# Weight splits of the first segments moved to ScalarE and GpSimd, and a third set of score operands, in a four-layer attention and Fourier kernel

## The chip, the core and the metric

One NeuronCore of a Trainium2 chip runs the whole program. Its engines each follow their own instruction stream and wait for each other through semaphores: TensorE (PE) multiplies matrices into PSUM, VectorE (DVE) and ScalarE (ACT) work on SBUF and PSUM, GpSimd (POOL) on SBUF only, and SyncE (SP) issues the DMAs. The metric is the device time of one execution in microseconds, the lower the better; the kernel is compared by the median of several executions.

## What is computed

`x` has 2048 rows of 512 values. Two kinds of layers alternate, twice each, and every layer adds to `x`:

```python
x = x + A(layernorm(x)); x = x + B(layernorm(x))
x = x + A(layernorm(x)); x = x + B(layernorm(x))

def A(x):            # 32 heads of width 16; the sequence in 4 segments of 512 rows
    for s in range(4):
        qs, ks, vs = the segment's q, k, v          # x @ wq, x @ wk, x @ wv
        a_dot = softmax(qs @ ks.T / 4 + causal mask) @ vs
        a_mem = (phi(qs) @ M) / (phi(qs) @ z + 1e-6)  # phi(t) = t+1 if t>0 else exp(t)
        outs.append(g * a_mem + (1 - g) * a_dot)      # g = sigmoid(beta)
        M = M + phi(ks).T @ vs;  z = z + sum(phi(ks))
    return concat(outs) @ wo

def B(x):            # Fourier mixing, real part
    a, b = x @ dft_hid_re.T, x @ dft_hid_im.T
    return dft_seq_re @ a - dft_seq_im @ b
```

## The kernel before

**Numbers.** Matrix products with float32 operands are made of float16 halves. Each weight matrix is scaled by a power of two taken from its largest magnitude and split into a high half (rounded to float16) and a low half (what the rounding lost); a product is then three matmuls, high by high, high by low and low by high (`mm3`). The scale needs a chain of its own: `absmax` reduces along the row on VectorE, `scales` transposes the result on TensorE, takes the maximum over partitions, and spreads it with a second matmul. `split` makes the halves: ScalarE writes the high one from `src` and the scale `s`, and VectorE the low one with a single scalar_tensor_tensor, (`src` × `s`) − high.

**Attention.** The 32 heads are cut into four groups of eight (`NG`), and the work is numbered by `i`, segment by segment and group by group: 4 groups × 4 segments × 2 layers = 32. For each `i`: `s_p` projects q and k with the group's weights; `t_split` makes halves of them and sends these through DRAM into the operand tiles `qst[i % NR]` and `kst[i % NR]`; `s_x` multiplies q by k for the row maxima, which VectorE takes from PSUM (`t_max`, in the profile the operation whose output is named `junk`, with `mx` behind it); a transpose of `mx` ends them, and four small DMAs put the negative maxima into `qst` as extra rows; `s_st` makes the scores, `t_sel` exponentiates them on ScalarE and masks them with an affine select on GpSimd; `s_av` multiplies them by v, from `vt[i % NR]`; `s_m` divides and merges (`t_merge`, with a round trip of denominators and reciprocals through DRAM), and `s_mem` keeps the memory. `NR` = 2, so two sets of operand tiles: `t_split` waits for the scores of group `i` − 2 before it writes the operands of group `i`, and `s_v` for that group's memory update and attention sum before it writes `vt`.

**Constant rows.** Rows 32 to 63 and 96 to 127 of `qst` and `kst` are filled once (`s_k`), `qst` with zeros by GpSimd, `kst` by VectorE: zeros, and an added column `pf` that puts 8192 in two rows of each half, which multiply the maxima's rows of `qst`. `t_split` and `s_x` overwrite the other rows of these blocks.

**Weights at the start.** `y` is the tile in which the Fourier layers sum their result; before that its pieces serve as staging room for the weights. The DMAs of the query and key weights of group 0 follow those of the first four tiles of `x`. `s_w` then goes through the groups: reductions and scales of query and key, the factors `f_q`, `f_k`, `f_k2` and `f_s`, the split of the query and the key weights, and a store of each to DRAM (`wqkv`), from which later segments load them. In group 0 it then waits for the layer norm of the first four tiles (`L`), issues all other weight loads and takes the scale of the value weights (`WL`); the value weights come last in each group. `s_wo` loads the output weights after `WL`, and the Fourier hidden weights (`wd`) after group 3's query and key (`W`); it makes the scales and 4 + 8 splits, after which `WO` lets the output projection (`s_o`), the hidden transform (`s_ab`) and the loads of the sequence matrices (`s_r`) begin.

**The order.** All of these are Python generators that yield what they need next: an engine, tiles, and slots from a shared pool of 2 KB per partition (`NW` = 50 slots, named `w` in the profile; PSUM banks are `b`; `g` holds the normalised, transposed rows). A planner (`Plan`) keeps an estimate of every engine's and tile's time with written-down costs, and always takes the step that can start first, with fixed priority among equals: so the instruction order of every engine is settled when the program is built, and any change of a cost, a slot count or a wait can change the order of everything behind it. `tt` chooses between VectorE and GpSimd for a tensor_tensor: it adds 8 ns per element to VectorE's planned free time and 2 to GpSimd's, and takes the smaller. Slots have limits per kind; at most three query or key weight tiles (`wt`) and two value tiles (`wv`) are held at once.

Every engine call passes through one helper, so nearly all instructions in the profile stand under line 247; they are told apart by tile names.

Of the kernel before, what the change touches and what calls it, by code (L numbers as in the profile page):

```python
# [1 line left out]

# [19 lines left out]
HG = H // NG  # L22
NP = HG // 2
LAYERS = 2
NW, NB = 50, 2
PAIRS = NT // 2
CHUNKS = [2] * 8
LATE = [(5, 0, 8), (6, 0, 4), (7, 0, 4), (5, 8, 12), (6, 4, 8), (7, 4, 8), (5, 12, 16), (6, 8, 12), (7, 8, 12),
# [8 lines left out]
RESERVE = dict(G=500.0, Y=1000.0, V=0.0, A=0.0)  # L37
BATCH = 4
FIRST = "cc", "craw"
NR = 2  # L40


class Plan:
# [99 lines left out]
    def op(self, eng, name, args, kw):  # L143
# [7 lines left out]
        if eng == "T":  # L151
            n, w = out[0].free_size(), aps[1]
            slow = 4 if w.dtype == F32 else 1
            c = n / 2.4 * slow + (18 if w.dtype == F32R else 3)
            cols = n * slow * w.partition_size() / 128
            mode, unit = "m", 0
            if name == "matmul" and out[0].partition_size() == 32:
                mode, unit = "v", out[0].start_partition() // 32
            elif w.partition_size() <= 64:
                mode, unit = "h", w.start_partition() // 64  # L160
        elif eng == "A":
            c = n / 1.2 + (52 if src else 93) + (93 if any(a.free_size() == 1 for a in ins) else 0)
        elif eng == "V":
            c = 68 + n / 0.96
            if name == "reciprocal":
                c = 68 + n * 6.25
            elif name == "scalar_tensor_tensor" and out[0].dtype == F32:
                c += 60
            elif name == "tensor_copy" and out[0].dtype == F16:
                c = 68 + n / 1.92  # L170
            elif name == "tensor_scalar" and out[0].dtype == F32:
                c = 68 + n / (0.87 if src else 1.32)
        elif eng == "G":
            c = 127 + n * 0.915 if name == "affine_select" else 96 + n * 2.2
# [79 lines left out]
def body(ctx: ExitStack, tc: tile.TileContext, x, wq, wk, wv, wo, beta, wd, cs, out):  # L254
# [38 lines left out]

    load(0, 0)
    load(0, 1)
    macc = const.tile([128, NG, 2, 4, 32], F32, name="macc")
    pl.fine[macc.tensor.name] = 256
    jp = macc[:, 0, 0].rearrange("p j d -> p (j d)")
# [86 lines left out]
    def flat(t):  # L385
        return t.rearrange("p a b -> p (a b)")

    def s_w():
        def part(n, g):
            i = 2 * g + n if n < 2 else 8  # L390
            yield need("A", tag="wv" if n == 2 else "wt")
            w = sb("wv" if n == 2 else "wt", F16, (128, 2, KT, 128))
            yield from split(w, stage[g][n], scl[:, i:i + 1])
            yield need("Y", w)
            Y.dma_start(wqkv[g][n], w)
            wnow[n, g] = w
            done.add(("W", n, g))

        for g in range(NG):
            for n in range(2):  # L400
                yield need("V", stage[g][n])
                absmax(2 * g + n, flat(stage[g][n]))
            yield from scales(2 * g, 2 * g + 2)
# [4 lines left out]
            yield from part(0, g)  # L408
            yield from part(1, g)
            if g == 0:  # L410
                yield gate(*[("L", 0, t) for t in range(TT)])
                Y.dma_start(gb[:, 0, :], beta)
                for j in range(NG):
                    load(j, 2)
                    if j:
                        load(j, 0)
                        load(j, 1)
                for j in range(NG):
                    yield need("V", stage[j][2])
                    V.tensor_reduce(vm[:, j:j + 1], flat(stage[j][2]), axis=AX.X, op=OP.max,  # L420
                                    apply_absolute_value=True)
                V.tensor_reduce(amax[:, 8:9], vm, axis=AX.X, op=OP.max)
                yield from scales(8, 9)
                done.add("WL")
            yield from part(2, g)

    def s_wo():
        wos = y[:, 12:16, :]
        yield gate("WL")
        Y.dma_start(wos, wo.rearrange("(t p) n -> p t n", p=128))  # L430
        yield gate(("W", 0, 3), ("W", 1, 3))
        wds = y[:, 0:8, :].rearrange("p (t e) n -> p t (e n)", e=2)
# [12 lines left out]
        V.tensor_scalar(f_o, inv[:, 8:9], inv[:, 9:10], 2.0 ** 9, op0=OP.mult, op1=OP.mult)  # L445
        V.tensor_scalar(f_y, inv[:, 10:11], 2.0 ** 9, None, op0=OP.mult)
        for k in range(KT):
            yield from split(w_o[:, :, k], wos[:, k], scl[:, 9:10])
        for e, s in enumerate((scl[:, 10:], sneg)):
            for k in range(KT):  # L450
                yield from split(w_d[:, :, k, 512 * e:512 * e + 512], wds[:, k, 512 * e:512 * e + 512], s)
        done.add("WO")

    def s_k():
# [3 lines left out]
            V.tensor_copy(f, t)  # L458
            V.tensor_scalar(f, f, scale, None, op0=OP.mult)

        pz = const.tile([128, 1], I32, name="pz")
        pf = const.tile([128, 1], F32, name="pf")
        yield need("V")
        V.tensor_scalar(pz, pi, 62, None, op0=OP.bitwise_and)
        V.tensor_copy(pf, pz)
        V.tensor_scalar(pf, pf, 62.0, 8192.0, op0=OP.is_equal, op1=OP.mult)
# [732 lines left out]
```

## Time and profile before

| | |
|---|---|
| runs of the kernel | 1785.94, 1790.37, 1789.98 us; median 1789.98 |
| the profiled execution | 1784.85 us |
| its span, first to last instruction | 1783.1 us |
| mean granted TensorE clock | 0.979 |
| busy: PE, DVE, ACT, POOL | 1676.0, 1111.9, 898.7, 723.1 us (94, 62, 50, 41% of the span) |
| DMA | 242.44 MB, 48.3% of 16 engines' span on SP's queue |

How to read the rows: in the summary by slices each digit is the busy share of one fortieth of the span, in tenths (for PEclk the granted clock, in tenths of full speed). In the views of single instructions the columns are start, duration (both in us), engine, line, operation, output and inputs by tile name with buffer numbers left out, shape, and count, then in brackets the idle time of the engine before it and what ended that. In the rows of groups the numbers behind the bar are busy time in us and the mean of one in ns, then the engine's idle time before these instructions. Matmul ends are modelled, and rows that stand for several instructions give the time from the first one's start to the last one's end.

### The profile page before, as it was taken

What the parts mean: (1) busy time and instruction counts of PE and PEld (TensorE: products, weight loads), DVE (VectorE), ACT (ScalarE), POOL (GpSimd) and SP (SyncE); (2) the same over time, 40 slices, a digit from 0 to 9 for tenths busy, and PEclk for the clock granted to TensorE, in tenths of its full rate; (3) what the DMA queues carried; (4) which work ended last, traced back from release to release, by engine and by line L of the source; (5) the groups of instructions that cost most, each with busy time, mean ns of one, the idle gap of its engine ahead of it and who ended that gap; (6) DMA issues with size and microseconds to landing.
All of it is one profiled execution on the core that took longest, in us unless ns stands there. A gap on an engine that the chain in (4) does not pass through costs nothing.

```text
span 1783.1 us, 32611 instructions
## 1 busy us (share of the span) xinstructions
PE 1676.0 (94%) x11029; PEld 731.7 (41%) x11029; DVE 1111.9 (62%) x3440; ACT 898.7 (50%) x1563; POOL 723.1 (41%) x1154
## 2 busy tenths in 40 slices
PE   3877899999999999999899998999999999999999
PEld 1432444443444444444444443444344434444444
DVE  7797865867596687455577757555756476533222
ACT  2547668666557667733437663565445544531000
POOL 3225455546454455543435544353624343331000
PEclk8888899999999999999999999999999999999999
DMA  7345645565465554345774772355424453227104
GB/s 195 99 124 134 176 118 140 163 176 149 124 182 150 148 129 134 106 123 165 221 222 156 199 181 73 95 139 149 122 81 119 131 133 87 83 92 230 53 0 136
DMA packets 240984, 242.44 MB, mean 136 GB/s; under 512 B 129776, under 2 KB 152304, under 8 KB 240816
## 3 DMA queue, kind: packets, MB, share of 16 engines
q1 hardware_dynamic: 240816, 240.35, 48.3%
q8 instruction: 87, 1.43, 0.3%
q14 instruction: 81, 0.66, 0.1%
HBM read 152.96 MB, written 63.70 MB: 122 GB/s over the span
## 4 chain that ended last, share of the span: by engine, by line
PE 59%; DVE 12%; DMA 12%; issue 5%; POOL 5%; ACT 4%; SPq 3%; POOLq 0%; DVEq 0%; ACTq 0%
PE b L247 59%; ACT w L247 4%; DVE junk L247 4%; POOL w L247 4%; DMA w<-w 3%; DVE w L247 3%; SPq L247 3%; DMA dc<-den 2%; DMA w<-rec 1%; DMA w<-in_cs_dram 1%; DMA den<-w 1%; DVE cam L247 1%; DMA w<-x 1%; DVE y L247 1%; DMA rec<-dc 1%
## 5 line engine op out<-in xcount | busy, mean ns | idle before, releaser
L247 PEld LDWEIGHTS <-w 128*128 128x128 f16 x4992 | 464.9, 98 | 624.6 <-issue 118.4
L247 PE MATMUL b<-w,w 128*128 128x512 f16 x3072 | 707.9, 380 | 5.8 <-POOL w L247 3.7
L247 POOL TENSOR_TENSOR w<-w,w 128x512 f16<-128x512 f32 (+1 forms) x317 | 381.2, 1208 | 372.9 <-ACT w L247 236.0
L247 ACT ACTIVATE w<-b,fac 128x512 f32<-128x512 f32 (+1 forms) x728 | 420.9, 657 | 207.8 <-PE b L247 193.1
L247 DVE CUSTOM_DVE_ANT_0 junk<-b,cmask 128x128 bf16<-128x128 f32 (+3 forms) x1024 | 438.4, 484 | 50.4 <-PE b L247 49.7
L247 POOL TENSOR_SCALAR_AFFINE_SELECT w<-w 128x128 f32<-128x128 f32 (+2 forms) x704 | 244.1, 359 | 364.4 <-ACT w L247 358.7
L247 DVE SCALAR_TENSOR_TENSOR y<-b,fyu,y 128x512 f32<-128x512 f32 x232 | 173.3, 747 | 215.9 <-PE b L247 214.5
L247 ACT ACTIVATE w<-b 128x512 f32<-128x512 f32 (+1 forms) x240 | 137.5, 599 | 176.1 <-PE b L247 171.1
L247 ACT ACTIVATE w<-w,csc 128x512 f16<-128x512 f32 (+1 forms) x256 | 181.7, 721 | 56.5 <-DVE csc L247 42.6
L247 PE MATMUL b<-g,w 128*128 128x512 f16 x768 | 186.7, 386 | 8.8 <-issue 5.3
L247 PE MATMUL b<-w,vt 128*32 128x512 f32 (+3 forms) x2048 | 176.7, 446 | 3.8 <-POOL w L247 2.8
L247 PE MATMUL b<-wd,w 128*128 128x512 f16 x768 | 179.9, 380 | 0.0
L247 DVE SCALAR_TENSOR_TENSOR w<-b,w 128x512 f16<-128x512 f32 x128 | 87.9, 687 | 131.5 <-ACT w L247 128.0
L247 ACT ACTIVATE w<-w 128x512 f16<-128x512 f32 (+1 forms) x144 | 90.1, 631 | 157.0 <-DVE w L247 116.1
L247 PE MATMUL b<-kst,qst 62*128 62x128 f16 (+3 forms) x1024 | 128.9, 307 | 15.3 <-DVE mx L247 7.1
L247 PE MATMUL b<-qst,kst 64*128 64x512 f16 (+3 forms) x1024 | 117.5, 305 | 8.6 <-ACT w L247 4.0
L247 PE MATMUL b<-w,g 128*128 128x128 f16 x1536 | 98.0, 221 | 9.6 <-DMA w<-w 4.4
L247 PEld LDWEIGHTS <-g 128*128 128x128 f16 x1536 | 88.8, 99 | 25.9 <-issue 16.0
L247 PEld LDWEIGHTS b<-w,vt 128*32 128x32 f32 x2048 | 53.9, 109 | 94.9 <-issue 53.2
L247 PE MATMUL b<-wo,w 128*128 128x512 f16 x384 | 89.8, 390 | 1.1 <-ACT w L247 0.9
L247 DVE TENSOR_REDUCE cam<-w 128x1 f32<-128x512 f32 x128 | 81.4, 675 | 11.2 <-DMA w<-in_cs_dram 11.0
L247 DVE DVE_READ_ACCUMULATOR2_ANT mx<- 128x1 f32 x1024 | 84.0, 82 | 0.0
(103 smaller groups left out, 841.0 us busy)
## 6 DMA issues: line engine op xcount, KB each, us to landing
w<-in_cs_dram SPq DMA_DIRECT2D x128, 256.0 KB
cc<-w SPq DMA_DIRECT2D x128, 256.0 KB
w<-cc SPq DMA_DIRECT2D x128, 256.0 KB
w<-w SPq DMA_DIRECT2D x96, 256.0 KB
d<-w SPq DMA_DIRECT2D x128, 128.0 KB
w<-rec SPq DMA_DIRECT2D x56, 256.0 KB
w<-in_x_dram SPq DMA_DIRECT2D x32, 256.0 KB
qst<-d SPq DMA_DIRECT2D x64, 128.0 KB
```

The source lines that it names most:

```text
L247: r = f(*args, **kw)
```

## The change

Five parts go together.

1. `split2` is new. ScalarE writes the high half, then scales `src` in place; the low half is a plain subtraction, handed to VectorE or GpSimd by `tt`. It takes the place of `split` everywhere but for group 0's query and key weights: 10 splits of query, key and value weights, 4 of the output weights and 8 of the Fourier weights.
2. The order of `s_w`: group 1's query and key weights are loaded beside group 0's, before the layer norm's transposes are issued; one chain of `scales` serves both groups; the four splits of groups 0 and 1 come first. All value weights and the query and key weights of groups 2 and 3 are loaded after the layer norm; their eight reductions come together, with one chain of `scales` for them and the value weights, and then eight splits in a fixed order.
3. `s_wo` waits for group 1's maxima (`("X", 1)`) as well before it loads the output weights.
4. `NR` goes from 2 to 3: a third `qst`, `kst` and `vt`. The room comes from the DMA scratch of the program, set to 1024; `NW` goes from 50 to 52.
5. The constant rows of `kst` are a memset on GpSimd with a float32 that holds two float16 8192; the column `pf` and VectorE's work for it go. Rows of these blocks that used to be zero now hold 8192. The planner's cost of a GpSimd memset or iota is written down as 80 + 0.9 per element.

```diff
-NW, NB = 50, 2
+NW, NB = 52, 2
...
-NR = 2
+NR = 3
+K8192 = struct.unpack("<f", b"\x00\x70" * 2)[0]
...
-            c = 127 + n * 0.915 if name == "affine_select" else 96 + n * 2.2
+            c = 127 + n * 0.915 if name == "affine_select" else 80 + n * 0.9 if name in ("memset", "iota") else 96 + n * 2.2
...
     load(0, 0)
     load(0, 1)
+    for n in range(2):
+        load(1, n)
...
-        dg = rg("dg", 3, F32, (128, 4))
+        dg = rg("dg", 3, F32, (128, 8))
...
+    def split2(o, src, s):
+        yield need("A", src, s)
+        A.activation(o[:, 0], src, AF.Copy, scale=s)
+        A.activation(src, src, AF.Copy, scale=s)
+        yield need("VG", o, src)
+        tt(o[:, 1], src, o[:, 0], OP.subtract)
+
     def s_w():
-        def part(n, g):
+        def part(n, g, how):
...
-            yield from split(w, stage[g][n], scl[:, i:i + 1])
+            yield from how(w, stage[g][n], scl[:, i:i + 1])
...
+        for g in range(2):
+            for n in range(2):
+                yield need("V", stage[g][n])
+                absmax(2 * g + n, flat(stage[g][n]))
+        yield from scales(0, 4)
+        for n in range(2):
+            yield from part(n, 0, split)
+        factors(0)
+        factors(1)
+        for n in range(2):
+            yield from part(n, 1, split2)
+        yield gate(*[("L", 0, t) for t in range(TT)])
+        for g in range(NG):
+            load(g, 2)
+        for g in range(2, NG):
+            for n in range(2):
+                load(g, n)
+        Y.dma_start(gb[:, 0, :], beta)
+        for g in range(NG):
+            yield need("V", stage[g][2])
+            V.tensor_reduce(vm[:, g:g + 1], flat(stage[g][2]), axis=AX.X, op=OP.max, apply_absolute_value=True)
+        V.tensor_reduce(amax[:, 8:9], vm, axis=AX.X, op=OP.max)
+        for g in range(2, NG):
+            for n in range(2):
+                yield need("V", stage[g][n])
+                absmax(2 * g + n, flat(stage[g][n]))
+        yield from scales(4, 9)
+        done.add("WL")
+        factors(2)
+        factors(3)
+        for x in ((2, 0), (0, 2), (1, 2), (2, 1), (2, 2), (0, 3), (1, 3), (2, 3)):
+            yield from part(*x, split2)
...
     def s_wo():
-        yield gate("WL")
+        yield gate("WL", ("X", 1))
...
-            yield from split(w_o[:, :, k], wos[:, k], scl[:, 9:10])
+            yield from split2(w_o[:, :, k], wos[:, k], scl[:, 9:10])
...
-                yield from split(w_d[:, :, k, 512 * e:512 * e + 512], wds[:, k, 512 * e:512 * e + 512], s)
+                yield from split2(w_d[:, :, k, 512 * e:512 * e + 512], wds[:, k, 512 * e:512 * e + 512], s)
...
         for i in range(NR):
-            for t, e in ((qst[i], G), (kst[i], V)):
+            for t, c in ((qst[i], 0.0), (kst[i], K8192)):
                 for a in range(2):
                     r = slice(64 * a + 32, 64 * a + 64)
-                    yield need(e.key)
-                    e.memset(t[r].rearrange("r p n -> r (p n)").bitcast(F32), 0.0)
-                    if e is V:
-                        yield need("V", pf)
-                        V.tensor_scalar(t[r], t[r], pf[r], None, op0=OP.add)
+                    yield need("G")
+                    G.memset(t[r].rearrange("r p n -> r (p n)").bitcast(F32), c)
...
-    nc = _bacc.Bacc("TRN2", target_bir_lowering=False, num_devices=1)
+    nc = _bacc.Bacc("TRN2", target_bir_lowering=False, num_devices=1, dynamic_dma_scratch_size=1024)
```

More of the change, by code (lines that the diff above doesn't have):

```diff
@@ L1 @@
+import struct
 from contextlib import ExitStack
@@ L397, in part, with factors @@
             done.add(("W", n, g))
[L399 to L403, printed above, removed]
+        def factors(g):
             for f, n, e in ((f_q, 0, -10), (f_k, 1, -10), (f_k2, 1, 12)):
@@ L407, in s_w @@
                             op0=OP.mult, op1=OP.mult)
[L408 to L425, printed above, removed]
+        for g in range(2):
[30 more added lines that the diff above has]
+            yield from part(*x, split2)
     def s_wo():
         wos = y[:, 12:16, :]
-        yield gate("WL")
+        yield gate("WL", ("X", 1))
         Y.dma_start(wos, wo.rearrange("(t p) n -> p t n", p=128))
@@ L459, in bits @@
             V.tensor_scalar(f, f, scale, None, op0=OP.mult)
[L461 to L466, printed above, removed]
         for i in range(NR):
-            for t, e in ((qst[i], G), (kst[i], V)):
+            for t, c in ((qst[i], 0.0), (kst[i], K8192)):
                 for a in range(2):
                     r = slice(64 * a + 32, 64 * a + 64)
-                    yield need(e.key)
-                    e.memset(t[r].rearrange("r p n -> r (p n)").bitcast(F32), 0.0)
-                    if e is V:
-                        yield need("V", pf)
-                        V.tensor_scalar(t[r], t[r], pf[r], None, op0=OP.add)
+                    yield need("G")
+                    G.memset(t[r].rearrange("r p n -> r (p n)").bitcast(F32), c)
             done.add(("QI", i))
```

## The prediction

> **What bounds the kernel now.** I read the page's summary by slices first, then the busy time by stage, then the first 230 us instruction by instruction.
>
> ```profile
> PE   3877899999999999999899998999999999999999
> DVE  7797865867596687455577757555756476533222
> PEclk8888899999999999999999999999999999999999
> ```
>
> Each digit is a 44.6 us slice. TensorE is below nine tenths, and its granted clock below full, in the first five slices; from then on it is the bound nearly everywhere. The next view puts numbers to it: the columns are the stretch, its length, then the busy time of PE, weight loads, DVE, ACT and POOL, the granted clock and the DMA share.
>
> ```profile
> 0.00:20.00 20.00, 1.21 (x4) 0.72 (x5) 17.40 (x47) 5.13 (x7) 12.93 (x20) 1.00 0.59 145
> 20.00:45.00 25.00, 13.79 (x92) 8.31 (x92) 16.31 (x66) 4.18 (x8) 2.46 (x2) 0.73 0.85 231
> 45.00:90.00 45.00, 40.17 (x320) 18.85 (x321) 32.97 (x130) 24.66 (x45) 10.71 (x24) 0.89 0.39 105
> 90.00:135.00 45.00, 34.67 (x241) 15.28 (x241) 41.45 (x164) 20.28 (x39) 12.13 (x26) 0.85 0.39 116
> 135.00:180.00 45.00, 33.10 (x224) 11.40 (x224) 30.76 (x75) 33.50 (x61) 23.91 (x44) 0.85 0.52 137
> 180.00:225.00 45.00, 37.90 (x265) 18.50 (x265) 37.60 (x145) 27.69 (x49) 21.16 (x31) 0.85 0.63 178
> 225.00:1740.00 1515.00, 1475.76 (x9708) 640.99 (x9705) 923.40 (x2803) 783.22 (x1360) 639.80 (x1008) 1.00 0.48 134
> 1740.00:1784.00 44.00, 39.41 (x183) 17.68 (x181) 12.01 (x16) 0.00 (x0) 0.00 (x0) 1.00 0.41 138
> ```
>
> Length less PE's busy time is PE's idle time: 18.8, 11.2, 4.8, 10.3, 11.9 and 7.1 us, together 64.1 us before 225 us, against 39.2 us in the 1515 us after it and 4.6 at the end. Busy time times (1 − clock) bounds what the lower clock cost in the five stretches from 20 us: 3.7, 4.4, 5.2, 5.0 and 5.7, together 24 us. So about 88 us are lost in the first eighth of the span, and that is where this change works. What is late there is told by the transposes that end each group's maxima (one per group of eight heads) and by group 1's weights.
>
> ```profile
> 56.55 0.40 PE L247 MATMUL b<-identf,mx 128*32 128x128 f32 x1 [3.70 <-DVE mx L247]
> 98.22 0.39 PE L247 MATMUL b<-identf,mx 128*32 128x128 f32 x1 [3.91 <-DVE mx L247]
> 129.14 0.28 PE L247 MATMUL b<-identf,mx 128*32 128x128 f32 x1 [0.39 <-DVE mx L247]
> 157.14 0.28 PE L247 MATMUL b<-identf,mx 128*32 128x128 f32 x1 [1.52 <-DVE mx L247]
> 202.20 0.40 PE L247 MATMUL b<-identf,mx 128*32 128x128 f32 x1 [3.14 <-DVE mx L247]
> 42.33 1.03 PE L247 MATMUL b<-kst,qst 62*128 62x128 f16 x12
> 45.52 0.71 ACT L247 ACTIVATE w<-y,scl 128x512 f16<-128x512 f32 x1
> 56.41 0.75 DVE L247 SCALAR_TENSOR_TENSOR w<-y,scl,w 128x512 f16<-128x512 f32 x1
> 56.74 4.05 PE L247 MATMUL b<-g,w 128*128 128x512 f16 x9
> 19.75 7.04 PE L247 MATMUL b<-g,w 128*128 128x512 f16 x24 [5.26 <-issue]
> ```
>
> Group 0's maxima run from 42.33 to 56.55, some 14 us, all on DVE; the next groups end 41.7, 30.9 and 28.0 us apart. ACT had rounded group 1's query weights by 45.5 or earlier, but their low halves waited in DVE's queue behind group 0's maxima until 56.41, so group 1's projection starts only at 56.74. Group 0's started at 19.75, and PE stood mostly idle in between. From group 1 on, each group's weights again go through DVE while maxima fill it.
>
> **The change part by part.** The prices:
>
> ```profile
> L247 DVE SCALAR_TENSOR_TENSOR w<-y,scl,w 128x512 f16<-128x512 f32 x12 | 9.7, 812 | 1.4 <-ACT w L247 1.4
> L247 DVE SCALAR_TENSOR_TENSOR wo<-y,scl,wo 128x512 f16<-128x512 f32 x4 | 3.6, 906 | 0.1
> L247 DVE SCALAR_TENSOR_TENSOR wd<-y,scl,wd 128x512 f16<-128x512 f32 x4 | 3.3, 832 | 0.0
> L247 DVE SCALAR_TENSOR_TENSOR wd<-y,sneg,wd 128x512 f16<-128x512 f32 x4 | 3.0, 744 | 0.0
> L247 ACT ACTIVATE w<-w,csc 128x512 f32<-128x512 f32 x4 | 2.9, 721 | 0.1
> L247 POOL TENSOR_TENSOR w<-w,w 128x512 f16<-128x512 f32 x14 | 16.7, 1193 | 11.7 <-ACT w L247 10.5 <-PE b L247 1.2
> L247 DVE TENSOR_REDUCE amax<-y 128x1 f32<-128x512 f32 x8 | 5.1, 671 | 0.0
> L247 POOL MEMSET qst<- 32x1024 f32 x4 | 3.8, 956 | 0.2
> L247 DVE MEMSET kst<- 32x1024 f32 x4 | 3.6, 912 | 1.0 <-issue 1.0
> L247 DVE TENSOR_SCALAR kst<-kst,pf 32x2048 f16<-32x2048 f16 x4 | 3.0, 747 | 0.1
> ```
>
> *Weight splits.* Of 24 splits, two (group 0's query and key) stay as they are. The other 22 lose a DVE operation: 10 × 0.812 + 4 × 0.906 + 4 × 0.832 + 4 × 0.744 = 18.0 us off DVE. Each gains a second, in-place scaling on ACT (22 × 0.721 = 15.9 us) and a subtraction that the planner gives to whichever of DVE and POOL it reckons freer; its rule counts 8 per element for DVE and 2 for POOL, so I take POOL for all: 22 × 1.193 = 26.2 us. One split then takes 0.72 + 1.19 us after its rounding instead of 0.81, 1.1 us longer; that is hidden wherever the weights are a projection ahead, and costs up to 1.1 us per group where they are not.
>
> *Constant rows of the operand tiles.* kst's memset and add leave DVE: 4 × (0.912 + 0.747) = 6.6 us. With a third set POOL fills 12 blocks instead of 4: 8 × 0.956 = 7.6 us more, in its gaps. Over 0 to 225 us, summing the stage rows, DVE goes from 176.5 to about 152 us, ACT from 115.4 to 131, POOL from 83.3 to 117: no engine but PE is near full.
>
> *First loads and scales.* Group 1's two loads move ahead of the layer norm's transposes on SP, and two more reductions (2 × 0.671 = 1.3 us) ahead of the first scales. The rows of that place:
>
> ```profile
> 11.72 0.91 DVE L247 MEMSET kst<- 32x1024 f32 x1 [0.27 <-issue]
> 12.67 0.55 DVE L247 TENSOR_SCALAR w<-w,mv,rs 128x512 f32<-128x512 f32 x1
> 13.96 1.68 POOL L247 TENSOR_TENSOR w<-w,w 128x512 f16<-128x512 f32 x1 [1.20 <-ACT w L247]
> ```
>
> The fourth tile's normalisation stood behind a kst memset (0.91), which goes; against it, a POOL memset (0.96) can stand before any of POOL's steps and the reductions take 1.3. Between −1 and +2.3 us; I take 0. SP's queue behind the norm has eight loads left in place of ten, so group 0's stores follow a little sooner; I count nothing.
>
> *Groups 1 to 3 earlier.* Group 1's weights need only the first scales and an ACT and a POOL that are nearly empty from 20 to 45 us (4.2 and 2.5 us busy). Its projection, two runs of the 24 matmuls of group 0 (7.04 us for 24, here the first run: 14 us for both, allowing for the clock), then fills PE's hole from 27 us on. Group 2's and 3's reductions come ahead of group 0's maxima, so their splits no longer meet DVE at all. Group 0's maxima start as before; group 1's follow at once, not 20 us later. The third operand set lets group 2's stores go without waiting for group 0's scores, which is what keeps DVE fed after group 1. Of the loss by stage (idle plus clock) I take back 7 of 14.9 in 20 to 45, 5 of 9.2 in 45 to 90, 9 of 15.5 in 90 to 135, 8 of 16.9 in 135 to 180 and 4 of 12.8 in 180 to 225: 33 of 69 us, since the maxima, the reciprocal's round trips through DRAM and the wait for the Fourier weights remain. Bounds: 10 if only group 1's own hole closes, 50 if PE is kept fed from 45 us.
>
> *Output and Fourier weights.* wo's load now waits for group 1's maxima too:
>
> ```profile
> 36.29 0.42 SPq L247 DMA_DIRECT2D y<-in_wo_dram  x1
> 99.23 0.43 SPq L247 DMA_DIRECT2D y<-in_wd_dram  x1
> 213.82 5.34 PE L247 MATMUL b<-wo,w 128*128 128x512 f16 x24
> ```
>
> It was loaded at 36.3 and first used after the Fourier weights' load at 99.2, so it has over 60 us of cover; if group 1's maxima stayed at 98 the cover would be just gone, at a price of a load (2 to 3 us). The first use of wo on PE is at 213.8; what brings groups 2 and 3 forward brings this forward, and from then on PE has filler.
>
> *Charges.* 22 subtractions in POOL's queue stand ahead of the affine selects that the attention sums wait for; some will be late by one subtraction. Zero to 22 × 1.193 = 26 us; nearest the low end, as POOL keeps half its time free: 4 us.
>
> *After 225 us.* Three sets and two more shared slots relax waits in a stretch whose idle time is 39.2 us, but every instruction is planned anew. Between −10 and +10 (a quarter of that idle time either way); I take 0.
>
> The sum against the profiled execution: 1784.85 − 33 + 4 = 1756. The median of the runs, 1789.98, is 5 us above the profiled one, the lowest run 1 us; I add half the gap: **1758 us**.
>
> **A row and a rule against the change.**
>
> ```profile
> 5.97 0.54 DVE L247 TENSOR_SCALAR w<-w,mv,rs 128x512 f32<-128x512 f32 x1
> 7.25 1.15 POOL L247 TENSOR_TENSOR w<-w,w 128x512 f16<-128x512 f32 x1 [0.33 <-ACT w L247]
> 7.43 1.25 DVE L247 TENSOR_SCALAR w<-w,mv,rs 128x512 f32<-128x512 f32 x1
> ```
>
> The same DVE operation takes 0.54 us alone and 1.25 when it starts under a POOL subtraction, ending just after it. So each moved subtraction can cost DVE 0.71 us: 22 × 0.71 = 15.6 us at most, if each meets such an operation; the maxima, most of DVE's work here, read PSUM. The Trainium skill, "SBUF — State Buffer", section "SBUF: two separate sides", calls the port pair of VectorE and GpSimd an exclusive lock, held for a whole instruction, which binds VectorE only in its two-port modes or with two SBUF inputs. The trace agrees for this operation; by that rule a maximum would not be held, and no run here shows that yet.
>
> **The rivals.**
> 1. *A small gain.* Matmul work paces the first segment, not weights: from group 1 on the maxima end 30.9 and 28.0 us apart with PE 75% busy. Then only the first two terms count: −12 + 4, that is 1777, and 1779 as a median. Against it: 10 us of idle per 45 us stretch.
> 2. *Slower, by POOL and DVE colliding.* The subtractions stand before the selects and hold DVE: the 15.6 us of stalls fall on the path, and 12 of the 22 splits (wo, wd) come 1.1 us later each, 13 us, putting off PE's filler. It decides once POOL is the later one in 135 to 225 us; now it is busy 45.1 of 90 us there. Its price, 28.6, less the 12 of the first two terms: 1801, 1804 as a median.
> 3. *Nothing.* The sets do not matter, and the new plan idles PE later by what it won before: the 39.2 us after 225 would have to grow by some 30. Then 1784 to 1790. That whole engines' orders change speaks for it; that every wait there gets looser speaks against.
>
> **How the numbers follow.** Forecast 60%, with its own range of 1742 to 1774 (49 or 17 us of recovery, charges 4); rival 1 20%; rival 2 12%; rival 3 8%. A difference under 0.3%, 5.4 us, can't be told from none. Faster: 60 + 19 + 2 = 81%; same: 1 + 5 + 1 = 7%; slower: 12%. The range takes in rivals 1 and 3 above and, below, a recovery of 50 with 10 us more after 225 us, which would be 1731 and of which I leave out the last 2: 1733 to 1788.
>
> **What would show it.** Right: group 1's projection begins before 40 us; group 1's maxima end by about 75 us in place of 98.2, group 3's by 130 in place of 157.1; PE's idle time before 225 us falls from 64 to 40 us or less; wo is first used near 185. Wrong: maxima still 28 us apart (rival 1); affine selects late behind POOL subtractions and DVE operations stretched past 1.2 us (rival 2); more than 50 us idle between 225 and 1740 (rival 3).

## The result and the profile after

The changed kernel takes 1784.13 us (median of 21 runs, 1777.5 to 1789.27) against 1787.6 us for the kernel before (21 runs, 1780.17 to 1792.7): a ratio of 0.9986, 95% interval 0.9974 to 0.9998. The forecast of 1758 us, a gain of 1.5%, did not come; the difference is no larger than what a measurement of this kernel can just tell from none. The profiled span is 1782.6 us, against 1783.1. In the profile after, the helper's line is 249 in place of 247.

The summary by slices of the kernel after:

```profile
PE   4978799999999999999899998999999999999999
DVE  7783777477667775545577656754676566342222
PEclk9978899999999999999899999999999999999999
```

The second slice of PE rises from 8 to 9 and the fourth from 7 to 8, but the third stays at 7 and the fifth falls from 8 to 7. DVE falls from 7 to 3 in its fourth slice (134 to 178 us) and from 8 to 4 in its eighth. How much that is, the same stretches as in the prediction tell (length, then busy time of PE, weight loads, DVE, ACT and POOL, the granted clock, the DMA share):

```profile
0.00:20.00 20.00, 2.84 (x8) 1.32 (x9) 14.67 (x45) 7.78 (x11) 15.55 (x22) 1.00 0.70 183
20.00:45.00 25.00, 17.87 (x128) 10.64 (x127) 20.07 (x57) 11.05 (x20) 12.36 (x13) 0.86 0.94 242
45.00:90.00 45.00, 42.19 (x371) 21.94 (x370) 33.73 (x154) 26.16 (x47) 17.82 (x31) 1.00 0.43 114
90.00:135.00 45.00, 34.12 (x246) 10.39 (x245) 38.83 (x145) 30.23 (x55) 24.64 (x54) 0.77 0.45 133
135.00:180.00 45.00, 38.00 (x271) 19.32 (x263) 17.75 (x44) 33.46 (x61) 21.37 (x33) 0.89 0.66 149
180.00:225.00 45.00, 34.54 (x230) 13.91 (x225) 35.88 (x143) 28.22 (x50) 26.75 (x38) 0.79 0.62 172
225.00:1740.00 1515.00, 1468.31 (x9613) 638.99 (x9612) 913.18 (x2788) 774.48 (x1347) 636.96 (x996) 0.99 0.48 133
```

Length less PE's busy time, plus busy time times (1 − clock), is each stage's loss, as in the prediction:

| stage | loss before | loss after | taken back | predicted |
|---|---|---|---|---|
| 20 to 45 | 14.9 | 9.6 | 5.3 | 7 |
| 45 to 90 | 9.2 | 2.8 | 6.4 | 5 |
| 90 to 135 | 15.5 | 18.7 | −3.2 | 9 |
| 135 to 180 | 16.9 | 11.2 | 5.7 | 8 |
| 180 to 225 | 12.8 | 17.7 | −4.9 | 4 |

Up to 90 us the change does what was predicted, 11.7 us against 12. From 90 to 225 it loses 2.4 us where a gain of 21 was expected. Behind 225 us PE is idle for 46.7 us in place of 39.2: 7.5 us more. With 1.6 us won before 20 us, the balance is 1.6 + 11.7 − 2.4 − 7.5 = 3.4 us won. The ratio says 2.5 us (0.14%), the two profiled spans 0.5; the clock behind 225, 0.99 in place of 1.00, is too coarse a figure to put into this sum. Instructions of PE, among them the transposes that end each group's maxima, show where the lead goes (start, duration, engine, operation; idle time and its end in brackets):

```profile
18.12 11.86 PE L249 MATMUL b<-g,w 128*128 128x512 f16 x45 [2.60 <-DMA g<-w]
...
59.58 0.27 PE L249 MATMUL b<-identf,mx 128*32 128x128 f32 x1
...
85.48 0.27 PE L249 MATMUL b<-identf,mx 128*32 128x128 f32 x1
...
113.19 0.40 PE L249 MATMUL b<-identf,mx 128*32 128x128 f32 x1 [4.56 <-DVE mx L249]
...
140.46 0.27 PE L249 MATMUL b<-identf,mx 128*32 128x128 f32 x1
...
179.79 0.40 PE L249 MATMUL b<-qst,kst 64*128 64x128 f16 x8
...
182.52 0.61 PE L249 MATMUL b<-kst,qst 62*128 62x128 f16 x12
...
201.16 0.39 PE L249 MATMUL b<-identf,mx 128*32 128x128 f32 x1 [6.45 <-DVE mx L249]
...
202.46 7.32 PE L249 MATMUL b<-wo,w 128*128 128x512 f16 x24
```

Both first projections are one run of 45 matmuls from 18.1 us; group 1's began at 56.7 before. The maxima of groups 1 to 3 end 12.7, 15.9 and 16.7 us earlier. Their distances are 25.9, 27.7 and 27.3 us, so the lead stops growing after group 1. Then it is lost in one step: group 4's maxima end at 201.16, 1.0 us before the old 202.20. Its first maxima matmul starts at 182.52, right behind the last scores of group 3 (179.79). From 135 to 180 us DVE, which takes the maxima, is busy for 17.75 us (30.76 before); behind 182 PE waits for it (6.45 us before the transpose at 201.16).

### The profile page after: what moved, and what is told of

Read it like the earlier page. It is cut to its first block, busy times and chain, and to the rows that moved or that the text cites. A ratio compares the mean times of both kernels' runs of the same rounds, so it can differ in the third digit from the quotient of the medians.

```text
span 1782.6 us, 32540 instructions
## 1 busy us (share of the span) xinstructions
PE 1676.7 (94%) x11020; PEld 733.9 (41%) x11020; DVE 1086.1 (61%) x3387; ACT 911.4 (51%) x1585; POOL 755.4 (42%) x1187
## 4 chain that ended last, share of the span: by engine, by line
PE 67%; DMA 11%; DVE 7%; ACT 5%; POOL 4%; issue 4%; SPq 2%; POOLq 0%; ACTq 0%; DVEq 0%
PE b L249 67%; ACT w L249 5%; POOL w L249 3%; DMA w<-w 3%; DVE w L249 2%; SPq L249 2%; DVE junk L249 2%; DMA dc<-den 2%; DMA w<-rec 2%; DMA w<-in_cs_dram 1%; DVE cam L249 1%; DVE bst L249 1%; DMA w<-in_x_dram 1%; DVE y L249 0%; DMA d<-w 0%
## 5 line engine op out<-in xcount | busy, mean ns | idle before, releaser
L249 ACT ACTIVATE w<-b 128x512 f16<-128x512 f32 (+1 forms) x240 | 137.9, 597 | 178.7 <-PE b L249 172.3
L249 PE MATMUL b<-kst,qst 62*128 62x128 f16 (+3 forms) x1024 | 124.7, 305 | 18.1 <-ACT w L249 5.6
L249 PE MATMUL b<-qst,kst 64*128 64x512 f16 (+3 forms) x1024 | 121.1, 304 | 13.3 <-ACT w L249 7.7
L249 PEld LDWEIGHTS <-g 128*128 128x128 f16 x1536 | 89.7, 99 | 26.9 <-issue 17.7
L249 PEld LDWEIGHTS <-kst 64*128 64x128 f16 x1024 | 37.5, 94 | 124.5 <-issue 118.8
```

Source lines behind the costliest of these rows:

```text
L249: r = f(*args, **kw)
```

## The experiments

Each kernel was compared with the kernel before on the same chip. Idle times are PE's, in us, from the same stretches as above.

| kernel | sets, slots | ratio (95%) | idle 0–90 | 90–225 | 225–1740 | group 4's maxima end |
|---|---|---|---|---|---|---|
| before | 2, 50 | 1 | 34.8 | 29.3 | 39.2 | 202.2 |
| the change | 3, 52 | 0.9986 (0.9974–0.9998) | 27.1 | 28.3 | 46.7 | 201.2 |
| wsplit | 3, 52 | 0.9974 (0.9958–0.9991) | 26.5 | 29.3 | 40.4 | 197.0 |
| nr2 | 2, 52 | 0.9946 (0.9930–0.9962) | 29.8 | 26.2 | 38.6 | 192.7 |
| nw50 | 3, 50 | 1.0065 (1.0050–1.0080) | 26.2 | 34.0 | 49.3 | 202.3 |
| sw | 2, 50 | 1.0024 (1.0009–1.0040) | 32.8 | 25.0 | 41.8 | 194.1 |
| nudge_before | 2, 50 | 1.0016 (0.9999–1.0034) | 34.7 | 27.6 | 42.2 | 196.7 |
| nudge2_before | 2, 50 | 1.0019 (1.0003–1.0035) | 35.8 | 25.6 | 39.0 | 211.3 |
| nudge_after | 3, 52 | 1.0033 (1.0010–1.0056) | 28.1 | 28.6 | 50.1 | 201.6 |
| nudge2_after | 3, 52 | 1.0055 (1.0038–1.0072) | 26.2 | 30.3 | 45.7 | 202.1 |
| nudge3_after | 3, 52 | 1.0082 (1.0055–1.0109) | 26.3 | 30.1 | 47.9 | 202.9 |
| nudge_nr2 | 2, 52 | 0.9963 (0.9946–0.9981) | 29.1 | 27.1 | 43.0 | 194.4 |
| nudge2_nr2 | 2, 52 | 0.9936 (0.9911–0.9961) | 29.2 | 25.9 | 37.9 | 192.1 |
| nudge3_nr2 | 2, 52 | 0.9994 (0.9980–1.0008) | 29.4 | 19.9 | 41.3 | 196.9 |
| nw57 | 2, 57 | 1.0034 (1.0018–1.0051) | 27.9 | 26.6 | 47.4 | 193.0 |
| nudge_nw57 | 2, 57 | 0.9953 (0.9935–0.9970) | 28.0 | 26.7 | 40.8 | 192.5 |
| nopmax | 3, 52 | 0.9995 (0.9978–1.0012) | 26.2 | 29.0 | 40.3 | 199.6 |
| noround | 3, 52 | 1.0066 (1.0042–1.0091) | 26.3 | 26.5 | 53.1 | 189.8 |
| nox1 | 3, 52 | 1.0015 (0.9995–1.0036) | 26.9 | 24.6 | 43.3 | 197.2 |
| nox1_nr2 | 2, 52 | 1.0095 (1.0070–1.0121) | 29.8 | 28.0 | 49.6 | 206.0 |

### One part undone at a time

`wsplit` gives the output and Fourier weights their old split back, in the changed kernel; `nr2` takes the third set away; `nw50` the two slots; `sw` is the kernel before with the new order of `s_w` and its splits alone.

```diff
 wsplit
-            yield from split2(w_o[:, :, k], wos[:, k], scl[:, 9:10])
+            yield from split(w_o[:, :, k], wos[:, k], scl[:, 9:10])
...
-                yield from split2(w_d[:, :, k, 512 * e:512 * e + 512], wds[:, k, 512 * e:512 * e + 512], s)
+                yield from split(w_d[:, :, k, 512 * e:512 * e + 512], wds[:, k, 512 * e:512 * e + 512], s)
 nr2
-NR = 3
+NR = 2
 nw50
-NW, NB = 52, 2
+NW, NB = 50, 2
```

> The kernel after, with the 12 splits of output and Fourier weights back to the one VectorE operation. Theory 1 (the lead of 16.7 us that group 3's maxima have is lost because the low halves of these weights end at 203.6 us in place of 184.9 and hold back PE's filler): last low half near 185, first sequence-matrix load near 183 instead of 198.5, PE's idle time from 135 to 225 us down from 17 to about 8, total 8 to 12 us under the kernel after. Theory 2 (PE is the bound once it is fed; whatever is won before 225 us is given back by another plan behind it): weights end earlier, total within 3 us of the kernel after.

> The kernel after with two operand sets instead of three, everything else kept. If the third set carries the lead of the first segment, group 2's and 3's maxima end 10 us or more later than the 113.2 and 140.5 us of the kernel after and the total is 5 to 10 us above it; if the sets matter little, as rival 3 of the prediction had it, those ends move by under 5 us and the total stays within 3 us.

> The kernel after with 50 shared slots instead of 52. A change of this size should not act before 225 us, where few slots are held; it shows how far a new plan alone moves the time. Theory 1: within 3 us of the kernel after. Theory 2 (each new plan wins or loses several us after 225 us): idle time of PE from 225 to 1740 us differs from 46.7 us by 5 or more, in either direction, and the total with it.

> The kernel before with the new order of the query, key and value weights and their splits on ScalarE and GpSimd alone (two sets, 50 slots, kst filled by VectorE, output and Fourier weights as before). If this order is what moves the first segment, group 1's maxima end near 86 us (98.2 before, 85.5 after) and PE's idle time before 90 us falls from 35 to under 30. Theory 1 then has the whole lead kept to 225 us and a total 8 us or more under the kernel before; theory 2 a total within 3 us of it.

The old splits did not bring the weights forward: the last low half of `wd` came at 213.1 us, against 203.6 in the changed kernel, and `wo` was first used at 212.0; yet the time was 0.9974. Later weights, then, are not what costs. Without the third set the kernel is faster, 0.9946; without the two slots it is slower than before, 1.0065. The order of `s_w` alone ended the weight splits at 153.4, 50 us earlier, but `wo` was first used at 203.9 all the same, and the time was 1.0024. Taken one by one, the four seem to say that every part matters and that none agrees with another. That is the sign to ask how much a new order of the instructions makes by itself.

The expectations fared no better. `nr2` was to be 5 to 10 us above the changed kernel or within 3 us of it, and is some 7 us under it (0.40%). `nw50` moved the total by 14 us, but PE's idle time behind 225 by only 2.6, not by 5. In `sw` group 1's maxima end at 94.7 us, not near 86, and the idle time before 90 us is 32.8, not under 30.

### The same kernels, planned anew

The planner has a written-down latency of 197 ns for PE. One or two nanoseconds more or less change no work, no wait and no slot, only the order in which the planner finds steps first. The edit is the same for the three kernels; 198 is called nudge, 196 nudge2, 195 nudge3.

```diff
-    LAT = dict(T=197.0, V=150.0, A=165.0, G=100.0, Y=0.0)
+    LAT = dict(T=198.0, V=150.0, A=165.0, G=100.0, Y=0.0)
```

> The kernel before, its planner told 198 instead of 197 ns for TensorE's latency: no edit to what is computed, to any tile or wait, but another order of instructions. If a new plan alone moves the time (theory 2), the total differs from the kernel before by 4 us or more with PE's idle time after 225 us differing by as much; if the time follows the edits, it stays within 3 us.

> The kernel after with the same nudge of 1 ns in the planner. Same reading: theory 2 has the total 4 us or more off the kernel after in either direction, by idle time after 225 us; otherwise within 3 us.

> The kernel before with the same second nudge. With three plans of each kernel: if the change is worth something beyond the plan's luck, the mean of its three ratios lies under the mean of the three of the kernel before by more than the spread within each; theory 2 has the two means within 0.3% of each other.

> The kernel after with 196 instead of 197 ns for TensorE's latency in the planner, a second plan of the same work. Theory 2: another total, 3 us or more off at least one of the other two plans of the kernel after, by idle time after 225 us.

> The kernel after with 195 ns, a fourth plan with three sets. If the third set costs time: 0.998 of the kernel before or more, with over 44 us of PE's idle time from 225 to 1740 us. If luck: as likely below 0.997 as above.

> The kernel after with two operand sets (0.9946 of the kernel before) and the planner's 198 ns. If two sets are really better, it stays within 0.3% of that; if that was a lucky plan, it comes back to 0.998 or more.

> The kernel after with two operand sets and the planner's 196 ns, a third plan. If two sets are better by themselves: 0.997 of the kernel before or less again. If the first two plans were luck: 1.000 or more.

> The kernel after with two operand sets and the planner's 195 ns, the fourth plan on that side. If the third set costs time by itself: 0.997 of the kernel before or less, group 4's maxima ending at 195 us or earlier (201 to 202 with three sets). If the plans scatter whatever the sets: as likely 1.000 or more.

The kernel before was not run at 195.

| latency | before | the change | with two sets |
|---|---|---|---|
| 197 | 1 | 0.9986 | 0.9946 |
| 198 | 1.0016 | 1.0033 | 0.9963 |
| 196 | 1.0019 | 1.0055 | 0.9936 |
| 195 | | 1.0082 | 0.9994 |
| mean | 1.0012 | 1.0039 | 0.9960 |

A plan alone moves the time of the changed kernel by up to 0.96% (0.9986 to 1.0082), that of the two-set kernel by 0.58%, and that of the kernel before, in three plans, by 0.19%, under the 4 us that its first nudge set as a mark. Against that, one kernel that differs by 0.4% says nothing, and the single runs of the part before (`wsplit`, `nw50`, `sw`) can't be assigned to their edits. In these plans, though, one thing holds: with the third set the kernel is slower in all four rows, by 0.40, 0.70, 1.19 and 0.88%, mean 0.79% or 14 us; without it, it is faster than before in the three rows that have both, by 0.54, 0.53 and 0.83%, mean 0.63% or 11 us. The plans of one row share no more than a number, so the groups count for more than the rows: of the three-set plans only 0.9986 lies under the slowest two-set plan, 0.9994, and all two-set plans lie under all plans of the kernel before. By these means the change is a gain of some 11 us and a loss of some 14, and the kernel as it was changed is the most favourable of its own four plans. `nudge3_nr2` was expected at 0.997 or below, with group 4's maxima ended by 195 us, and came out at 0.9994 with 196.9: the two-set kernel scatters more than thought, and for a single plan the lead is not certain. Nor does it hold under every further edit: without the added wait of `s_wo` (`nox1` and `nox1_nr2` below, one plan each) the kernel with three sets stands at 1.0015 and the one with two at 1.0095.

### What the third set does to the order

In the stretches of the two-set kernel, `nr2`:

```profile
90.00:135.00 45.00, 35.57 (x259) 13.05 (x257) 38.08 (x155) 27.82 (x52) 21.82 (x49) 0.85 0.52 160
135.00:180.00 45.00, 38.17 (x283) 17.26 (x283) 22.74 (x76) 40.34 (x72) 30.46 (x45) 0.94 0.52 139
180.00:225.00 45.00, 35.09 (x223) 15.60 (x214) 36.44 (x132) 26.31 (x46) 23.85 (x34) 0.79 0.63 178
225.00:1740.00 1515.00, 1476.39 (x9704) 645.60 (x9703) 914.10 (x2778) 771.40 (x1344) 632.02 (x994) 0.99 0.47 134
```

PE is idle for 38.6 us behind 225, not 46.7, and DVE works 22.74 us between 135 and 180, not 17.75. Its group 4 on PE (first maxima matmul, end of the maxima), group 3's last scores between them:

```profile
163.51 0.21 PE L249 MATMUL b<-kst,qst 62*128 62x128 f16 x1
...
176.07 0.40 PE L249 MATMUL b<-qst,kst 64*128 64x128 f16 x8 [1.58 <-DVE w L249]
...
192.66 0.28 PE L249 MATMUL b<-identf,mx 128*32 128x128 f32 x1 [1.40 <-DVE mx L249]
```

The maxima of group 4 start 12.6 us before group 3's scores end, and are woven in between them. With three sets they start after all of those. That they could start sooner is told by SP's queue, where the operands are loaded into their tiles, first in the changed kernel and then in `nr2`:

```profile
148.26 1.84 SPq L249 DMA_DIRECT2D qst<-d  x4
158.71 1.81 SPq L249 DMA_DIRECT2D kst<-d  x4
160.62 1.75 SPq L249 DMA_DIRECT2D qst<-d  x4
...
170.62 1.79 SPq L249 DMA_DIRECT2D kst<-d  x4
```

```profile
150.41 1.74 SPq L249 DMA_DIRECT2D qst<-d  x4
...
156.14 1.82 SPq L249 DMA_DIRECT2D kst<-d  x4
...
176.48 1.73 SPq L249 DMA_DIRECT2D qst<-d  x4
178.25 2.41 SPq L249 DMA_DIRECT2D kst<-d  x4
```

The first pair is group 4's, the second group 5's, which with two sets has to wait for group 3's scores (176.07). With three, group 5's operands go 16 and 8 us earlier, and group 4's maxima begin 23.8 us after its keys were sent (158.71 to 182.52) instead of 7.4 (156.14 to 163.51). In the view of groups from 140 to 182 us the value projections tell the same; first the changed kernel, then `nr2`:

```profile
L249 PE MATMUL b<-w,g 128*128 128x128 f16 x96 | 5.7, 219 | 0.0
```

```profile
L249 PE MATMUL b<-w,g 128*128 128x128 f16 x48 | 2.8, 219 | 0.0
```

Two groups' value projections come in that time, not one. The pattern stands in all four plans of each kind: the first maxima matmul of group 4 at 182.1 to 183.6 with three sets and 163.5 to 167.2 with two, the end at 201.2 to 202.9 and 192.1 to 196.9, on average 7.9 us apart, although group 3's maxima ended at 140.5 to 141.8 in the former and only at 145.9 to 148.7 in the latter. So in these plans the third set let the planner prepare group 5 ahead of finishing group 4, and in the changed kernel DVE stood idle for 27 of the 45 us from 135 to 180. The order is shown. It is not forced by the third set alone: `wsplit`, with three sets and one plan, starts group 4's maxima at 172.1 and keeps DVE busy for 24.6 us from 135 to 180.

Nor are these 8 us what the third set costs in the end. They are not carried on: group 6's maxima end at 276.9 to 279.9 us in the four plans with three sets and at 270.9 to 283.5 in the four with two. And over all kernels the end of group 4's maxima does not go with the time: 189.8 in `noround`, at 1.0066, and 211.3 in `nudge2_before`, at 1.0019. Where the 14 us lie is told by the table of idle times, as means of the four plans of each kind:

| PE, us | three sets | two sets |
|---|---|---|
| idle 0 to 90 | 26.9 | 29.4 |
| idle 90 to 225 | 29.3 | 24.8 |
| idle 225 to 1740 | 47.6 | 40.2 |
| busy, whole span | 1679.6 | 1675.0 |

The third set saves 2.5 us up to 90 us, costs 4.5 from there to 225 and 7.4 behind it. Behind 225 all four plans with it (45.7 to 50.1) lie above all four without it (37.9 to 43.0), while the three plans of the kernel before average 40.1, like the two-set kernel. That the larger part is idle time behind 225 us is thus shown for these plans; which waits there the third set lengthens is not.

### Slots, and what holds back PE's filler

`nw57` gives the two-set kernel the room of the third set as five more slots. `nudge_nw57` is the same at 198.

> The kernel after with two operand sets and the third set's room given to five more shared slots, 57. If slots are what is short after 225 us, idle time of PE there falls under the 37 us that two sets with 52 slots showed (225 to 1740 us) and the total is 3 us or more under that kernel (1772); if a new plan only scatters, either sign, and the first 90 us are as with two sets and 52 slots.

> Two operand sets, 57 slots, the planner's 198 ns. If more slots cost what the third set costs (more work let in ahead of what is due), 1.001 or more again; if the first plan with 57 slots was bad luck, 0.997 or less, as with 52.

1.0034 and 0.9953: the two plans lie on both sides of no change, against 0.9946 and 0.9963 with 52 slots. Whether slots are worth anything stays open.

Four runs asked what decides the first use of the output weights, which was at 202.5 us and not at 185. `nopmax` leaves out ten of VectorE's twelve reductions over the output and Fourier weights, `noround` the division by the softmax denominators in the first segment, and the last two drop the added wait of `s_wo`, with three sets and with two.

```diff
 nopmax
-        for i in (12, 13, 14, 15, *range(8)):
+        G.memset(pm, 0.0)
+        for i in (12, 0):
 noround
+        short = key[0] == "o1" and key[1] < NG
...
-        for src in (e, o):
+        for src in () if short else (e, o):
...
 nox1, nox1_nr2
-        yield gate("WL", ("X", 1))
+        yield gate("WL")
```

> The kernel after, leaving out 10 of the 12 reductions that look for the largest output and Fourier weight (the other two stand for them): 6.7 us of VectorE's work gone between 95 and 129 us, where VectorE is full. If VectorE paces groups 2 and 3 there, group 3's maxima end 5 us or more before 140.5 and the output projection starts 5 us before 202.5; if TensorE or the chains of DMAs pace them, both move by under 3 us.

> The kernel after, leaving out the division by the softmax denominators in the first segment (groups 0 to 3): the round trip of denominators and reciprocals through DRAM goes from the chain that runs from group 3's maxima to the output projection. Theory 3 (PE's losses from 90 to 225 us hang on that chain, which the change leaves as long as it was): the output projection starts 8 to 14 us before 202.5 us, the first matmul of the hidden transform as much before 224.1, and PE's idle time from 90 to 225 us falls from 28.3 to 20 or less. Rival (VectorE or ScalarE paces these stages): starts within 3 us, idle time within 3 us.

> The kernel after without the wait for group 1's maxima ahead of the output weights' load. If the late weights hold back the filler: Fourier splits end before 165 us instead of 203.6, the first sequence-matrix load is issued near 160 to 170 instead of 198.5, the output projection starts before 198 us and PE's idle time from 90 to 225 us falls under 25 (28.3); total 4 us or more under the mean of the plans of the kernel after (1.0025 of before). If the chain from group 3's maxima sets it: weights are split earlier, the output projection stays at 200 or later and the idle time within 3 us.

> The same with two operand sets. If late weights cost time there too (Fourier splits ended at 189.0 with two sets), total under 0.9946 of the kernel before; if the chain sets the filler, the output projection stays within 3 us of 203.8 and the total scatters around 0.995.

Less work on VectorE did not help: group 3's maxima ended at 145.9, later than 140.5, and `wo` was used at 215.4. In `noround`, PE's first matmuls with the output weights:

```profile
218.99 6.29 PE L249 MATMUL b<-wo,w 128*128 128x512 f16 x18
```

come later too, although group 4's maxima end at 189.8. They start about when the last low half of `wd` is made (219.4; 203.6 in the changed kernel, where `wo` came at 202.5). There the weights look like the gate; in `sw`, with the splits done 50 us ahead, they can't have been. So no single gate is shown: the planner put the freed time into other steps, and whichever chain was left then ended last. Without the wait the output weights are loaded at 39.6 us, not 89.9, and in `nox1` the maxima of group 3:

```profile
169.72 0.27 PE L249 MATMUL b<-identf,mx 128*32 128x128 f32 x1
```

end 29 us later than with it. The last low half of `wd` is made at 150.2 there, and `wo` is first used only at 217.0: early weights did not bring it forward. The total is 1.0015, within the scatter of plans; with two sets it is 1.0095, outside what four plans with the wait showed (0.9936 to 0.9994). With one plan of each, no more can be said than that no gain from dropping the wait was seen.

### The best version

The changed kernel with two sets is faster than both kernels in most of its plans; `nudge2_nr2`, with the latency at 196, is the fastest that ran, 1771.7 us and 0.9936 (0.9911 to 0.9961). Its two stretches that differ most from the changed kernel's:

```profile
135.00:180.00 45.00, 39.50 (x289) 17.90 (x290) 23.91 (x82) 41.20 (x73) 30.77 (x46) 0.89 0.54 144
...
225.00:1740.00 1515.00, 1477.12 (x9731) 646.23 (x9728) 914.25 (x2779) 771.17 (x1343) 632.11 (x992) 1.00 0.47 135
```

PE is busy for 8.8 us more behind 225 than in the changed kernel (1477.12 against 1468.31). Part of that is the execution: the profile is of the fastest of its six runs. The choice of 196 over 197 is luck of the plan; the choice of two sets rests on the eight plans above.

## The prediction, step by step

**What bounds the kernel** was read rightly: the loss sat before 225 us, and the first two stages gave back what they were said to, 11.7 us for 12. Group 1's projection began with group 0's. The startup is a little better than 0: 1.6 us less idle.

**The work moved** is as costed. These are groups of the changed kernel, up to 230 us (busy time, mean ns):

```profile
L249 ACT ACTIVATE y<-y,scl 128x512 f32<-128x512 f32 x18 | 13.0, 722 | 0.6
L249 POOL TENSOR_TENSOR wd<-y,wd 128x512 f16<-128x512 f32 x8 | 9.2, 1157 | 1.0 <-ACT y L249 1.0
L249 POOL MEMSET qst<- 32x1024 f32 x6 | 5.8, 960 | 0.3
L249 POOL MEMSET kst<- 32x1024 f32 x6 | 5.7, 944 | 0.2
L249 DVE TENSOR_TENSOR wo<-y,wo 128x512 f16<-128x512 f32 x1 | 0.7, 693 | 3.4 <-ACT y L249 3.4
```

0.722 us for the in-place scaling (0.721 used), 1.157 for a subtraction on POOL (1.193), 0.95 for a memset block (0.956). DVE lost 25.8 us over the whole span (24.6 predicted), POOL gained 32.3 (33.8), ACT 12.7 (15.9). Three of the 22 subtractions went to DVE (the row of `wo`, and two of the query, key or value weights), so "POOL for all" was nearly right.

**Where it failed: "9 of 15.5 in 90 to 135, 8 of 16.9 in 135 to 180 and 4 of 12.8 in 180 to 225".** These 21 us rested on weights being what paces groups 2 and 3, and on maxima by 75 and 130. Weights paced group 1 and little else. All splits of the query, key and value weights are done by 54 us in the changed kernel, yet the maxima of groups 1 to 3 end at 85.5, 113.2 and 140.5 us (75 and 130 were forecast for the first and last), still 26 to 28 us apart, which is the sign of rival 1. PE's idle time before 225 us is 55.4 us, not 40. The stages behind 90 us lose as before: 45.2 us before, 47.6 after, and in `nr2` 9.4 + 5.3, 6.8 + 2.3 and 9.9 + 7.4, together 41.1. So even without the third set about 4 of the 21 came. Rival 1's price, −12 + 4, is near the mean gain of the two-set kernel, 11 us. Its reason, that matmul work sets the pace, is not shown. In the view of waits of the changed kernel from 60 to 141 us (total, times, longest), what PE waits for most is VectorE's maxima:

```profile
PE b L249 <- DVE mx L249: 8.7, 9, 4.6
```

VectorE is busy for 25.0 of the 27.3 us between the ends of group 2's and group 3's maxima (27.5 of 28.0 before), which "no engine but PE is near full", a mean over 225 us, did not show. But `nopmax`, with less work on VectorE, did not bring these ends forward, so what sets the pace stays open.

**The second failure: the third set as a help.** It "lets group 2's stores go without waiting for group 0's scores, which is what keeps DVE fed after group 1". It did let stores go, of group 5 before group 4's maxima, and DVE was fed less: 17.75 us in 135 to 180 against 22.74 with two sets (17.8 to 19.5 and 21.9 to 23.9 over the four plans of each; the 30.76 before hold weight splits too). "That every wait there gets looser speaks against" was the argument by which rival 3 got 8%; a list planner does not owe a looser wait a better order. The term after 225 us, 0 with bounds of ±10, measured a loss of 7.5: inside, but it took the bulk of what was won. So the time is rival 3's, and it needed not 30 us of new idle time but 7.5, since only 11 had been won before 225 us. Its reason, that the sets do not matter, is not what the runs show, and that the changed kernel still comes out a little ahead is the luck of its plan: its four average 1.0039.

**Rival 2** did not happen. The operation of its quoted row takes as long as before, under the same subtraction, in the changed kernel's instructions at the start:

```profile
7.18 1.15 POOL L249 TENSOR_TENSOR w<-w,w 128x512 f16<-128x512 f32 x1 [0.70 <-ACT w L249]
7.37 1.25 DVE L249 TENSOR_SCALAR w<-w,mv,rs 128x512 f32<-128x512 f32 x1
```

but a maximum was not stretched. Its groups in the first 225 us, in the kernel before and in the changed one:

```profile
L247 DVE CUSTOM_DVE_ANT_0 junk<-b,cmask 128x384 bf16<-128x384 f32 x44 | 21.9, 551 | 0.0
```

```profile
L249 DVE CUSTOM_DVE_ANT_0 junk<-b,cmask 128x384 bf16<-128x384 f32 x46 | 23.4, 551 | 2.6 <-PE b L249 2.5
```

The mean is 551 ns in both, though POOL's busy time in these stages rose from 83.3 to 118.5 us; the 16 of the 46 that run for more than half of their time under a POOL tensor_tensor of over 0.9 us average 553 ns. The maxima read PSUM and one mask in SBUF, so this agrees with the Trainium skill, "SBUF — State Buffer", section "SBUF: two separate sides", in that the lock binds VectorE in its two-port modes or with two SBUF inputs. Its other half, splits that come later, was there (the last of `wd` at 203.6), and no price of it shows: with the splits later still (`wsplit`) the kernel was not slower. **The wait for group 1's maxima** cost nothing that the runs show: loaded at 89.9, `wo` was needed at 202.5, and without the wait (`nox1`) later still.

**What stays open:** which waits behind 225 us the third set lengthens; what paces groups 2 and 3; which chain lets PE's filler begin; what a slot is worth. That two sets beat three in four plans of four is a small sample, with one pair 0.4% apart, and the one pair without the added wait goes the other way.

## What to carry to other kernels

When a planner settles every engine's order, run the old and the new kernel under two or three plans that differ by nothing but a nanosecond in a cost; their spread (here up to 1%) is the smallest effect that a single run of an edit can show. A stage's idle time belongs to the next thing that paces it, so take back only what the removed wait ended, and look at the distance of the repeated step (26 to 28 us here) for the rest. More buffers can let a greedy order run ahead with the next group before the last one is finished; look for the engine that goes hungry then.

## What the runs showed of the chip

PE's busy time for the same matmuls is not fixed, and it does not follow the mean granted clock alone. Two plans of the changed kernel, both profiled at a clock of 0.978, keep PE busy for 1675.24 us (`nudge_after`) and 1683.40 us (`nudge2_after`).

One execution in one order varies too. The profile of `nudge2_nr2` has a span of 1764.6 us at a clock of 0.981; four of its other five runs took 1769.5 to 1770.1 us at 0.975 to 0.976. So of the 18.0 us between this span and the changed kernel's (1782.6 us), some 5 are found between runs of the same order, and how much of a better order's gain comes back through the clock is not shown.
